# Attention readout and the first expert block of a fused kernel: four entries of a hand-written order moved

## The chip, the cores and the metric

The program runs on one core of one Trainium2 chip. The metric is the device time of one execution in microseconds; the median of the runs of the kernel before is 201.0 us (three runs, 200.04 to 203.24).

## What is computed

Two blocks run one after the other. The first is an attention with a polynomial sketch in place of the softmax. The second takes its output, row by row, to one of eight experts.

```python
def phi(x):                                   # r = 8, head_dim = 32
    a = np.einsum('rd,bhsd->bhsr', S1, x)
    b = np.einsum('rd,bhsd->bhsr', S2, x)
    return np.einsum('bhsi,bhsj->bhsij', a, b).reshape(*x.shape[:-1], r * r)
q_p, k_p = (phi(q), phi(k))                   # q, k, v: (4, 4, 1088, 32)
kv = np.einsum('bhsf,bhsd->bhfd', k_p, v)
z = np.sum(k_p, axis=2)
num = np.einsum('bhsf,bhfd->bhsd', q_p, kv)
den = np.einsum('bhsf,bhf->bhs', q_p, z)[..., None] + 1e-06
x = (num / den) -> rows of (B*S, H*D) = (4352, 128)
...
logits = xn @ en.T / tau;  expert_idx = argmax;  gate_w = softmax prob of that expert
for e in range(8):
    h = np.maximum(x[mask] @ w1[e], 0.0)      # w1: (8, 128, 1024)
    out[mask] = gate_w[mask, None] * (h @ w2[e])
```

## The kernel before, in words

The four batches are worked on in two pairs, number 0 and number 1. The rows of a pair are cut into four tiles of four chunks (named 0 to 3) and a rest (r). For keys and queries of each tile a step turns the tile on TensorE (`ktr`, `qtr`, line 427), sketches it (`kab`, `qab`), copies the sketch out of PSUM and multiplies the two halves into 64 features per head (`kp`, `qp`, line 464). The keys' features meet the values in `kv` (line 530). For the queries of pair 1 the features are turned back, so that features lie on partitions: `trqp` (line 642, TensorE, into PSUM) and `qpT` (lines 648 and 651, ScalarE, PSUM to SBUF). `nd` (line 664, TensorE) multiplies them with the summed keys and values into PSUM tile `ps_big`, which is called the readout here; `x` (lines 677 to 684, VectorE) divides by the denominator and writes the rows `xg` and their router logits. The diff's words are these: "query features turned" is `trqp` with `qpT`, and tile number 2 is the third tile; "second, third readout" are `nd 1 1` and `nd 1 2`.

Behind that come 35 blocks of 128 rows. Block i has its rows fetched by an indirect DMA (`fetch`, line 1047, GpSimd's queue), is turned on TensorE (`turn`, line 1057) and copied to SBUF as `xTb` (line 1059), multiplied with the first weights (`up`, line 1139, into `ps_big`), put through Relu by ScalarE (line 1147), multiplied with the second weights (`down`, lines 1177 and 1182) and scattered to the output (line 1195). `norm` (lines 1152 and 1153) and `shares` (line 1163) make its gate. The first ten blocks hold rows of pair 0 alone, so that block 0 can begin while pair 1 is still read out.

The order of the work on every engine is written out by hand. `HEAD` (line 400), `ORDER` (line 408) and `AFTER_TURN` (line 417) are lists of step names; each step's instructions are emitted in the order of the lists, and the steps of one block get a rank within the block's tick. Each engine runs its instructions in that order and waits where one of them needs a semaphore. The steps of `AFTER_TURN` stand behind the `up` of block 0 and the `turn` of block 1. Which instruction may start is also set by the pools of buffers:

```python
    def ps_small():
        return psum.tile([P, 512], F32, tag="t", bufs=2, name="ps_t")
    def ps_big():
        return psum.tile([P, 2, 512], F32, tag="big", bufs=2, name="ps_big")
...
    def tile_of(n, shape, tag):
        return work.tile(shape, F32, tag=tag if n > 1 else tag + "1",
                         bufs=2 if tag == "both" and n == 1 else 1 if n == 1 else
                         {"both": 4, "qT": 3, "kp": 3}.get(tag, 2), name=tag)
...
            elif c0 // 4 in TWO_BANKS:
                s["ps"] = [ps_one("acc"), ps_one("ab")]
```

So `nd` and `up` take turns in two PSUM buffers `ps_big`, and a new one waits until the reader of the one before the last has done. The turned features `qpT` of whole tiles have two buffers in SBUF. `trqp 2` and `trqp 3` both go through the one buffer `ps_acc` and the one buffer `ps_ab`, so that the later of them waits for ScalarE's copies of the earlier.

At the start of the program the two sketch matrices come in as words of 64-bit numbers, are put together on VectorE (`words`) and turned on TensorE (`sketches`, line 232); VectorE then writes three tiles from that (lines 233 to 236).

Of the kernel before, what the change touches and what calls it, by code (L numbers as in the profile page):

```python
# [72 lines left out]
def kernel(  # L73
# [324 lines left out]


    HEAD = """  # L400
constants; words; norm emb; one columns; clear 0; sketches; ktr0 0; qtr0 0; scale emb; kab0 0; kb0 0; turn emb; pairs 0; kp0 0;
place emb; sec 0 0; ktr0 1; sec 0 1; qtr0 1; prod 0 0; prod 0 1;
kab0 1; kb0 1; kp0 1; lane; ktr0 2; pairs 1; qtr0 2; sec 1 0; sec 1 1; prod 1 0; prod 1 1; ktr0 3; kab0 2; kb0 2;
kp0 2; lanes; qtr0 3; kv0 0; pairs 2; sec 2 0; sec 2 1; prod 2 0; prod 2 1; kab0 3; kb0 3; kp0 3; downs; ktr0 r; qtr0 r; kv0 1;
# [6 lines left out]
qab 0 t; qb 0; kv 3; best 0; place 0; count; qtr 3; qtr r; qp 0;  # L411
take 0; kv 2; kv r; qtr 2; trqp 0; total; split 0; trkv; qab 1 t; qab 3 ab; rest; mark 00; qb 1;
qab r ab; mark 01; find; exp0; kvT; qab 2 acc; sums; kve; qb 2; qpT 0; qb 3; qb r; qp 1; tokens; qp 3; kz;
trqp 1; nd 1 0; fetch0; fetch 1; qp 2; qp r; x 1 0; trqp 3; qpT 1; others; qpT 3; nd 1 1; x 1 1; trqp 2; norm 0; turn 0;
qpT 2; trqp r; qpT r"""
    AFTER_UP = ""
    AFTER_TURN = "nd 1 2; x 1 2; nd 1 3; x 1 3"
    steps = {}

    def turned(tiles, rest, n, tag, parts=1, big=False):  # L420
# [461 lines left out]
    def plan_early():  # L882

        full, upto, w = column("full"), column("upto0"), column("w_early")

        def count():
            tokens_by_expert(((less, ones),), full, spare[0][:, NC * E:(NC + 1) * E])

        def rest():
            nc.vector.tensor_tensor_scan(out=upto[:], data0=ones_e[:], data1=full[:], initial=0.0, op0=ALU.mult, op1=ALU.add)  # L890
            nc.vector.tensor_scalar(w, full, -1.0, float(KEYS), op0=ALU.mult, op1=ALU.add)
            first, early["expert_0"], early["experts"] = blocks(0, upto, w, lane)
            at = first()
            nc.vector.tensor_add(at, at, lane[:, :EARLY])
            early["key"] = at

        def others():
            nc.vector.tensor_scalar_min(c_early[:, 1:], upto, float(EARLY))
            early["took"] = column("took")
            nc.vector.tensor_sub(early["took"], c_early[:, 1:], c_early[:, :E])  # L900
        return count, rest, others
# [303 lines left out]
    def put_at(tick):  # L1205
        def put(after, rank, f):
            at.setdefault(tick + after, []).append((rank, len(at.get(tick + after, ())), f))
        put.tick = tick
        return put
# [11 lines left out]
    count, rest, others = plan_early()  # L1221
# [13 lines left out]
    for i, name in enumerate(x.strip() for x in ORDER.split(";")):  # L1235
        put_at(4)(0, 47.2 + 0.01 * i, steps[name])
    for at_, names in ((30.5, AFTER_UP), (46, AFTER_TURN)):
        for i, name in enumerate(x.strip() for x in names.split(";") if x):
# [3 lines left out]
    count, rest, shared, others, experts, number, start, extra = plan_late()  # L1242
# [118 lines left out]
```

## Time and profile before

| | |
|---|---|
| median of the runs | 201.0 us (200.04 to 203.24) |
| profiled execution, its own time | 200.79 us |
| its span, first to last instruction | 198.8 us |
| TensorE (PE) busy | 186.3 us, 94% of the span |
| ScalarE (ACT), GpSimd (POOL), VectorE (DVE) busy | 106.3, 103.7 and 90.6 us |
| mean granted TensorE clock | 0.991 |

The profile holds one execution. A row of its timeline gives the start on the span's clock, the time from there to the end of the row's last instruction, the engine (PEld is TensorE's weight load), the source line, the operation, output and inputs, how many instructions stand in the row, and in brackets how long the engine had been idle and what ended that. The ends of matmuls are modelled. A float32 matmul of the program stands as two in the trace, a transpose as one. "remote" in brackets means that the profile knows no instruction whose end released the waiting one.

### The profile page before, as it was taken

How to read it: one execution, taken by the hardware profiler on the slowest of the kernel's cores; microseconds unless marked ns; L12 is line 12 of the kernel's file. 1: busy time of each engine (PE TensorE's matmuls, PEld its weight loads, DVE VectorE, ACT ScalarE, POOL GpSimd, SP SyncE). 2: the span in 40 equal slices, each digit the busy share in tenths (PEclk: the TensorE clock that was granted, in tenths of full speed). 3: DMA queues.
4: the chain of work that ended last, by engine and by line, in shares of the span. 5: the costliest groups of instructions: out<-in, count | busy, mean ns of one | idle time of the engine just before them, and what ended most of it. 6: DMA issues, size and time to landing. Idle time of an engine off the chain costs nothing.

```text
span 198.8 us, 7202 instructions
## 1 busy us (share of the span) xinstructions
PE 186.3 (94%) x2701; PEld 176.5 (89%) x2701; DVE 90.6 (46%) x396; ACT 106.3 (53%) x293; POOL 103.7 (52%) x134
## 2 busy tenths in 40 slices
PE   8978999999579997999999999999999999999991
PEld 7657889998478997999999999999999998999990
DVE  6777877899336818994223122221312211123200
ACT  3664443246235517552366564556545596978850
POOL 5110029105715275384588878767687666732442
PEclk9999999999969999999999999999999999999999
DMA  5898999987460688634553979878699799694201
GB/s 142 230 307 232 325 246 296 316 282 200 129 261 0 167 285 325 214 124 129 162 154 83 279 189 277 219 228 231 170 281 273 218 326 230 174 329 108 95 26 33
DMA packets 42598, 41.22 MB, mean 207 GB/s; under 512 B 17625, under 2 KB 36066, under 8 KB 42562
## 3 DMA queue, kind: packets, MB, share of 16 engines
q1 hardware_dynamic: 40272, 36.06, 63.2%
q0 software_dynamic: 2240, 4.67, 7.3%
q8 instruction: 23, 0.38, 0.8%
q14 instruction: 13, 0.11, 0.2%
q10 hardware_dynamic: 50, 0.01, 0.0%
HBM read 34.69 MB, written 6.10 MB: 205 GB/s over the span
## 4 chain that ended last, share of the span: by engine, by line
PE 61%; DMA 18%; DVE 10%; another core or an unknown queue 4%; issue 2%; ACT 2%; SPq 1%; POOLq 1%; ACTq 0%; DVEq 0%
PE ps_big L1139 22%; DMA out_dram<-y,dst_i 12%; PE ps_ab L1177 10%; PE ps_acc L1177 9%; PE ps_big L664 5%; PE ps_acc L530 4%; DMA v<-in_v_dram 4%; DMA k<-in_k_dram 2%; DVE hits L848 1%; PE ps_t L855 1%; PE ps_t L427 1%; PE ps_big L1144 1%; DVE row L775 1%; PE ps_acc L1182 1%
## 5 line engine op out<-in xcount | busy, mean ns | idle before, releaser
L1139 PE MATMUL ps_big<-xTb,wb 128*128 128x128 f32 (+1 forms) x608 | 64.4, 279 | 4.9 <-ACT xTb L1059 4.6
L1139 PEld LDWEIGHTS ps_big<-xTb,wb 128*128 128x128 f32 (+1 forms) x608 | 60.7, 178 | 6.0 <-ACT xTb L1059 5.1
L1195 POOL DMA_INDIRECT out_dram<-y,dst_i x35 | 36.2, 1035 | 41.6 <-ACT sq L1152 11.8
L1147 ACT ACTIVATE hT<-ps_big 128x1024 f32<-128x1024 f32 x35 | 35.8, 1023 | 37.7 <-PE ps_big L1139 21.2
L1047 POOL DMA_INDIRECT xs<-rows,dst_i x35 | 35.6, 1018 | 18.8 <-DVE dst_i L872 11.2
L1166 DVE TENSOR_SCALAR gate<-gate 128x1 f32<-128x1 f32 x35 | 5.2, 148 | 54.0 <-ACT probs L1163 26.7
L1177 PE MATMUL ps_ab<-w_sb,hT 128*128 x208 | 25.6, 276 | 0.0
L1177 PE MATMUL ps_acc<-w_sb,hT 128*128 x208 | 25.4, 275 | 0.0
L1153 POOL TENSOR_TENSOR norm<-norm,half_c 128x1 f32<-128x1 f32 x35 | 21.5, 616 | 6.8 <-ACT sq L1152 6.4
L1177 PEld LDWEIGHTS ps_ab<-w_sb,hT 128*128 128x128 f32 x208 | 24.3, 192 | 0.1
L1177 PEld LDWEIGHTS ps_acc<-w_sb,hT 128*128 128x128 f32 x208 | 24.3, 192 | 0.0
L464 POOL TENSOR_TENSOR kp<-both 128x1024 f32<-128x1024 f32 (+1 forms) x3 | 4.5, 1512 | 16.8 <-ACT both L459 16.8
L1054 DVE STREAM_TRANSPOSE xTb<-held 128x128 f32<-128x128 f32 x22 | 9.2, 416 | 9.0 <-DMA held<-squares 8.1
L1115 ACT COPY v<-w_sb 128x1024 f32 x12 | 12.2, 1039 | 0.5 <-issue 0.4
L1188 ACT ACTIVATE y<-ps_ab,gate 128x128 f32<-128x128 f32 x17 | 6.2, 365 | 9.8 <-PE ps_t L1057 3.4
L1163 ACT ACTIVATE probs<-xs,norm 128x8 f32<-128x8 f32 x35 | 10.3, 296 | 1.3 <-DVE norm L1157 1.3
L1152 ACT ACTIVATE sq<-xs 128x128 f32<-128x128 f32 x35 | 10.6, 302 | 0.1
L1182 PE MATMUL ps_acc<-v,hT 128*64 128x128 f32 (+1 forms) x192 | 10.1, 274 | 0.2 <-issue 0.2
L1182 PEld LDWEIGHTS ps_acc<-v,hT 128*64 128x64 f32 (+1 forms) x192 | 8.8, 128 | 0.9 <-issue 0.4
L1188 ACT ACTIVATE y<-ps_acc,gate 128x128 f32<-128x128 f32 x17 | 6.2, 367 | 6.2 <-issue 3.3
L530 PE MATMUL ps_acc<-v,kp 128*64 128x64 f32 x224 | 7.6, 224 | 1.1 <-DMA v<-in_v_dram 1.1
L530 PEld LDWEIGHTS ps_acc<-v,kp 128*64 128x64 f32 x224 | 7.0, 138 | 1.8 <-issue 1.8
(279 smaller groups left out, 289.6 us busy)
## 6 DMA issues: line engine op xcount, KB each, us to landing
wb<-in_moe_w_dram SPq DMA_DIRECT2D x35, 512.0 KB
w_sb<-in_moe_w_dram SPq DMA_DIRECT2D x16, 256.0 KB
rows<-xg SPq DMA_DIRECT2D x4, 544.0 KB
v<-in_v_dram SPq DMA_DIRECT2D x4, 512.0 KB
k<-in_k_dram SPq DMA_DIRECT2D x3, 512.0 KB
q<-in_q_dram SPq DMA_DIRECT2D x3, 512.0 KB
v<-in_moe_w_dram SPq DMA_DIRECT2D x3, 512.0 KB
squares<-xs SPq DMA_DIRECT2D x22, 64.0 KB
```

What stands on the lines that cost most here:

```text
L530: nc.tensor.matmul(acc[m][u * HALF:(u + 1) * HALF, i, p], s["kp"][:, c - c0, h], bass.AP(tensor=vo.tensor, offset=vo.offset, ap=[list(vo.a ...
L1047: nc.gpsimd.indirect_dma_start(out=xs[i][:], out_offset=None, in_=rows[:2 * S if t == 0 else N + 1], in_offset=bass.IndirectOffsetOnAxis(a ...
L1115: nc.scalar.copy(to, w2_sb[:, bass.ds(e, 1)].rearrange("p o f d -> p (o f d)"))
L1139: nc.tensor.matmul(ps[c:c1, u, j * P:(j + 1) * P], w[:, f * P + c:f * P + c1], x, start=True, stop=True)
L1147: nc.scalar.activation(hT[i], ps, ACT.Relu)
L1152: nc.scalar.activation(sq, xs[i][:, :DM], ACT.Square, accum_out=norms[i])
L1153: nc.gpsimd.tensor_tensor(out=norms[i], in0=norms[i], in1=half_c, op=ALU.pow)
L1163: nc.scalar.activation(p, xs[i][:, DM:], ACT.Exp, scale=norms.pop(i)[:, 0:1], accum_out=gate[i])
L1177: nc.tensor.matmul(ps, h[:, f * P:(f + 1) * P], ws[0][:, f], start=f == 0, stop=f == NF - 1)
L1182: made = nc.tensor.matmul(ps[n0:n1], h[:, f * P + n0:f * P + n1], ws[int(two(i) and n0 > 0)][:, f], start=f == 0, stop=f == NF - 1, skip_g ...
L1188: y_made = nc.scalar.activation(y, ps, ACT.Copy, scale=gate.pop(i)[:, 0:1])
L1195: d = nc.gpsimd.indirect_dma_start(out=out[:, :], out_offset=bass.IndirectOffsetOnAxis(ap=dst_i[t][:, j:j + 1], axis=0), in_=y[:], in_offs ...
```

## The change

Four entries of the lists are moved; no instruction is added, taken away or altered.

```diff
     HEAD = """
-constants; words; norm emb; one columns; clear 0; sketches; ktr0 0; qtr0 0; scale emb; kab0 0; kb0 0; turn emb; pairs 0; kp0 0;
+constants; words; norm emb; one columns; clear 0; ktr0 0; sketches; qtr0 0; scale emb; kab0 0; kb0 0; turn emb; pairs 0; kp0 0;
 place emb; sec 0 0; ktr0 1; sec 0 1; qtr0 1; prod 0 0; prod 0 1;
...
 qab r ab; mark 01; find; exp0; kvT; qab 2 acc; sums; kve; qb 2; qpT 0; qb 3; qb r; qp 1; tokens; qp 3; kz;
-trqp 1; nd 1 0; fetch0; fetch 1; qp 2; qp r; x 1 0; trqp 3; qpT 1; others; qpT 3; nd 1 1; x 1 1; trqp 2; norm 0; turn 0;
-qpT 2; trqp r; qpT r"""
+trqp 1; nd 1 0; fetch0; fetch 1; qp 2; qp r; x 1 0; trqp 3; qpT 1; others; qpT 3; trqp 2; qpT 2; nd 1 1; x 1 1; trqp r; qpT r; norm 0; turn 0; nd 1 2; x 1 2"""
     AFTER_UP = ""
-    AFTER_TURN = "nd 1 2; x 1 2; nd 1 3; x 1 3"
+    AFTER_TURN = "nd 1 3; x 1 3"
```

On TensorE, from the readout `nd 1 0` (`ps_big_1099`) to the end of the readout of pair 1, the kernel before has this (L664 is a readout, L642 turns query features, L1057 turns a block's rows, L1139 is `up`; the first L1057 and the first L1139 belong to block 0):

```order
L664 MATMUL ps_big_1099<-kz1_208,qpT_1077 64x82 x16
L642 MATMUL ps_acc_1137<-ident_87,qp_1086 128x128 x4
L642 MATMUL ps_ab_1138<-ident_87,qp_1086 128x128 x4
L664 MATMUL ps_big_1156<-kz1_208,qpT_1147 64x82 x16
L642 MATMUL ps_acc_1180<-ident_87,qp_1126 128x128 x4
L642 MATMUL ps_ab_1181<-ident_87,qp_1126 128x128 x4
L1057 MATMUL ps_t_1194<-ident_87,xs_1116 128x128
L642 MATMUL ps_t_1201<-ident_87,qp_1128 128x128 x2
L1077 TENSOR_LOAD exp_0_213
L1139 MATMUL ps_big_1211<-xTb_1196,wb_1038 128x128 x8
L1057 MATMUL ps_t_1229<-ident_87,xs_1118 128x128
L664 MATMUL ps_big_1233<-kz1_208,qpT_1198 64x82 x16
```

In the changed kernel, whose source lines are one less, the same stretch reads:

```order
L663 MATMUL ps_big_1099<-kz1_208,qpT_1077 64x82 x16
L641 MATMUL ps_acc_1137<-ident_87,qp_1086 128x128 x4
L641 MATMUL ps_ab_1138<-ident_87,qp_1086 128x128 x4
L641 MATMUL ps_acc_1156<-ident_87,qp_1126 128x128 x4
L641 MATMUL ps_ab_1157<-ident_87,qp_1126 128x128 x4
L663 MATMUL ps_big_1169<-kz1_208,qpT_1147 64x82 x16
L641 MATMUL ps_t_1193<-ident_87,qp_1128 128x128 x2
L1056 MATMUL ps_t_1202<-ident_87,xs_1116 128x128
L663 MATMUL ps_big_1206<-kz1_208,qpT_1166 64x82 x16
L1076 TENSOR_LOAD exp_0_213
L1138 MATMUL ps_big_1235<-xTb_1204,wb_1038 128x128 x8
L1056 MATMUL ps_t_1253<-ident_87,xs_1118 128x128
```

The eight transposes of tile 2 now stand ahead of `nd 1 1`, and the 16 matmuls of `nd 1 2` ahead of the `up` of block 0, which had stood ahead of them. `nd 1 3` stays where it was, behind the `turn` of block 1.

On ScalarE the stretch between the copies of tile 3's turned features and the Relu of block 0 (L1147) reads, before:

```order
L651 COPY qpT_1153<-ps_acc_1137 128x512
L651 COPY qpT_1153<-ps_ab_1138 128x512
L1152 ACTIVATE sq_1190,norm_1191<-xs_1116 128x128
L1059 COPY xTb_1196<-ps_t_1194 128x128
L651 COPY qpT_1198<-ps_acc_1180 128x512
L651 COPY qpT_1198<-ps_ab_1181 128x512
L648 COPY qpT_1204<-ps_t_1201 128x256
L1147 ACTIVATE hT_1212<-ps_big_1211 128x1024
```

and with the change:

```order
L650 COPY qpT_1153<-ps_acc_1137 128x512
L650 COPY qpT_1153<-ps_ab_1138 128x512
L650 COPY qpT_1166<-ps_acc_1156 128x512
L650 COPY qpT_1166<-ps_ab_1157 128x512
L647 COPY qpT_1196<-ps_t_1193 128x256
L1151 ACTIVATE sq_1198,norm_1199<-xs_1116 128x128
L1058 COPY xTb_1204<-ps_t_1202 128x128
L1146 ACTIVATE hT_1236<-ps_big_1235 128x1024
```

The copy `xTb` of block 0 and the square for its norm have gone behind the three copies of turned features. On VectorE `x 1 2` goes ahead of the two instructions of block 0's norm, and nothing else moves. GpSimd's and SyncE's queues hold the same instructions in the same order. At the start of the program TensorE turns the first four key chunks (L427) ahead of the sketches (L232) instead of behind them.

## Rows read from the trace of the kernel before

**Rows 1.** The page's chain of waits: shares of the span by engine.
```profile
PE 61%; DMA 18%; DVE 10%; another core or an unknown queue 4%; issue 2%; ACT 2%; SPq 1%; POOLq 1%; ACTq 0%; DVEq 0%
```

**Rows 2.** Timeline of PE (start us, us, engine, line, operation, count, idle before), 48 to 63 us.
```profile
48.77 0.66 PE L642 MATMUL ps_acc<-ident,qp 128*128 128x128 f32 x4
49.79 1.37 PE L664 MATMUL ps_big<-kz,qpT 128*64 128x82 f32 x32
51.09 0.66 PE L642 MATMUL ps_acc<-ident,qp 128*128 128x128 f32 x4
...
52.02 0.27 PE L1057 MATMUL ps_t<-ident,xs 128*128 128x128 f32 x1
52.12 0.38 PE L642 MATMUL ps_t<-ident,qp 128*128 128x128 f32 x2
56.10 3.68 PE L1139 MATMUL ps_big<-xTb,wb 128*128 128x128 f32 x16 [3.59 <-ACT xTb L1059]
59.62 0.27 PE L1057 MATMUL ps_t<-ident,xs 128*128 128x128 f32 x1
59.82 2.79 PE L664 MATMUL ps_big<-kz,qpT 128*64 128x82 f32 x72
62.87 2.02 PE L1139 MATMUL ps_big<-xTb,wb 128*128 128x128 f32 x16 [0.25 <-PE ps_big L664]
```

**Rows 3.** Timeline of DVE, 54 to 56 us: `x 1 1` from first to last.
```profile
54.26 0.17 DVE L677 TENSOR_SCALAR rc<-ps_big 128x16 f32<-128x16 f32 x1 [2.97 <-remote]
...
55.37 0.28 DVE L683 TENSOR_TENSOR parts<-ps_big,rc 128x128 f32<-128x128 f32 x1
55.68 0.38 DVE L684 TENSOR_REDUCE lg<-parts 128x32 f32<-128x128 f32 x1
```

**Rows 4.** Timeline of ACT, 49 to 61 us.
```profile
49.52 0.59 ACT L651 COPY qpT<-ps_acc 128x512 f32<-128x512 f32 x1 [0.93 <-PE ps_acc L642]
50.00 0.59 ACT L651 COPY qpT<-ps_ab 128x512 f32<-128x512 f32 x1
50.48 0.32 ACT L1152 ACTIVATE sq<-xs 128x128 f32<-128x128 f32 x1
50.69 0.20 ACT L1152 ACTIVATION_READ_ACCUMULATOR sq<-xs 128x1 f32 x1
55.78 0.27 ACT L1059 COPY xTb<-ps_t 128x128 f32<-128x128 f32 x1 [4.89 <-remote]
...
56.90 0.40 ACT L648 COPY qpT<-ps_t 128x256 f32<-128x256 f32 x1
59.82 1.02 ACT L1147 ACTIVATE hT<-ps_big 128x1024 f32<-128x1024 f32 x1 [2.52 <-PE ps_big L1139]
60.74 0.26 ACT L1059 COPY xTb<-ps_t 128x128 f32<-128x128 f32 x1
```

**Rows 5.** Busy time in stretches: bounds, us; PE, PEld, DVE, ACT, POOL busy (count); clock, DMA share, GB/s.
```profile
52.60:56.00 3.40, 0.00 (x0) 0.00 (x0) 1.64 (x6) 0.22 (x2) 2.45 (x3) 1.00 0.89 292
56.30:59.50 3.20, 3.20 (x16) 3.20 (x17) 0.02 (x1) 1.00 (x3) 0.00 (x0) 0.50 0.59 216
...
63.00:194.00 131.00, 129.78 (x1615) 127.60 (x1617) 45.57 (x238) 77.37 (x215) 83.87 (x95) 1.00 0.69 201
15.60:24.00 8.40, 8.40 (x240) 6.94 (x242) 6.46 (x13) 3.42 (x10) 0.00 (x0) 1.00 0.93 271
```

**Rows 6.** Timeline of PE at the program's start.
```profile
4.32 0.28 PE L232 MATMUL ps_ab<-ident,srows 16*128 16x16 f32 x1
4.54 0.85 PE L427 MATMUL ps_t<-ident,k 128*128 128x128 f32 x4
5.22 0.61 PE L427 MATMUL ps_t<-ident,q 128*128 128x128 f32 x4
...
12.18 0.63 PE L427 MATMUL ps_t<-ident,q 128*128 128x128 f32 x4 [0.49 <-DMA q<-in_q_dram]
...
15.54 1.15 PE L530 MATMUL ps_acc<-v,kp 128*64 128x64 f32 x32 [1.09 <-DMA v<-in_v_dram]
```

**Rows 7.** Timeline of POOL, 53 to 55 us, with the norm and the sixth fetch.
```profile
53.50 0.58 POOL L1153 TENSOR_TENSOR norm<-norm,half_c 128x1 f32<-128x1 f32 x1
54.26 0.99 POOL L1047 DMA_INDIRECT xs<-rows,dst_i  x1 [0.18 <-issue]
```

**Rows 8.** Timeline of PE, 74 to 76 us: the only longer gap behind 63 us.
```profile
75.82 0.38 PE L1139 MATMUL ps_big<-xTb,wb 128*128 128x128 f32 x1 [1.02 <-ACT xTb L1059]
```

## The prediction

> **What bounds the kernel now.** I read the chain of waits first: 61% of it are work of PE, TensorE [rows 1], so what PE waits for is what counts. Then the timeline of PE, in which the reader is to see its one long wait [rows 2]: the last work in front of it starts at 52.12 us, the next at 56.10, and in the busy table PE does nothing at all from 52.6 to 56.0 [rows 5]. The `up` of block 0 that follows takes 3.68 us; the `up` of block 1, the same instructions, takes 2.02 [rows 2], and the granted clock in between is 0.50, which is 1.2 GHz instead of 2.4 [rows 5]. So this place costs 3.6 us of idle time and about 1.7 us of half clock. From 63 to 194 us PE is busy for 129.78 of 131.00 us [rows 5], and the one longer gap there is 1.02 us [rows 8]; what is won or lost before the `up` of block 1, which starts at 62.87, is carried to the end nearly whole. That start is the number I work out.
>
> Next I ask who holds PE. It waits for ScalarE's `xTb`, which runs at 55.78 after an idle time of 4.89 us, though the transpose that it reads started at 52.02 and took 0.27 [rows 2, 4]. VectorE's `x 1 1` begins at 54.26, after 2.97 us idle, though the readout it reads ended by its row at 49.79 + 1.37 = 51.16 [rows 2, 3]. Both are put down to "remote": both engines saw TensorE's signal some 3 us after the end that its rows give (54.26 - 51.16 = 3.1; 55.78 - 52.29 = 3.5). The profile doesn't say why. Everything below hangs on what becomes of these two late signals.
>
> **The change part by part.** *Sketches behind the first keys.* The sketches' transpose starts at 4.32, the keys' at 4.54, and the queries' follows at 5.22 [rows 6]. Exchanged, the keys start 0.2 us earlier and the sketches 5.22 - 4.54 = 0.7 us later, and VectorE's three tiles from them as well. What hides that: PE then waits 0.49 us for queries at 12.18 and 1.09 us for values at 15.54, both for DMAs that nothing here moves [rows 6]. Together 1.6 us of slack against 0.7: I count nothing. Without this cover it would cost 0.7; it can't gain, since the DMA at 15.54 ends the stretch either way.
>
> *Turning tile 2 ahead of `nd 1 1`.* It is the same eight transposes, so PE's work stays. But they need `ps_acc` and `ps_ab` free, and ScalarE's second copy of tile 3 ends at 50.00 + 0.59 = 50.59 [rows 4]. The last four transposes (about 0.45 us, from four in 0.5 in the row at 48.77) then end at 51.1, and `nd 1 1` (1.30 us from its start to the next row) at about 52.45 instead of 51.16. In its turn ScalarE may not write tile 2's turned features at once: they have the buffer that `nd 1 1` reads, of two, so all of ScalarE's queue behind them, block 0's square and `xTb` included, waits for the signal of `nd 1 1`.
>
> *From that signal to the first block.* ScalarE: two copies 0.48 + 0.59 = 1.07, the rest's copy 0.35, square and accumulator 0.41, `xTb` 0.26 [rows 4], together 2.1 us. PE meanwhile has the readout `nd 1 2` to do, 1.30 us, after the first 1.07. VectorE's `x 1 1` frees its PSUM buffer for `up` after 55.37 + 0.28 - 54.26 = 1.4 us [rows 3]; that fits below the 2.1. On GpSimd the norm of block 0 and, queued behind it, the sixth fetch [rows 7] come later by as much as the square; that block's `turn` is five ticks away, so nobody waits.
>
> *From `up` of block 0 to `up` of block 1.* Relu starts 0.05 us after `up` ends, and `xTb` of block 1 is done 0.92 + 0.26 = 1.2 us later [rows 4]. PE has a `turn` (0.1 us) and `nd 1 3` to do in that time: 40 of the 72 matmuls that take 2.79 us, so 1.6 us [rows 2]; the buffer that it writes is free once `x 1 2` has read it, 1.4 us after `nd 1 2`. So I take 1.7 us from the end of the one `up` to the start of the next (before: 62.87 - 59.78 = 3.1, with both readouts in it).
>
> *The sum.* I take it that the late signals come at the moments at which they came, 54.24 and 55.7: nothing that is moved is on the DMA queues or on GpSimd's queue up to there. ScalarE copies tile 2 from 54.3 to 55.35, PE does `nd 1 2` from 55.4 to 56.7, ScalarE copies the rest at 55.8 and has `xTb` ready at 56.8. `up` of block 0 runs from 56.85 to 58.65 at full clock, and `up` of block 1 starts at 58.65 + 1.7 = 60.35: 2.5 us earlier than 62.87. The clock is the disputed term. The longest idle stretch of PE falls from 3.6 to 55.4 - 52.7 = 2.7 us. The rows have a gap of 1.09 us with the clock still at 1.00 behind it [rows 5, 6], and one of 3.6 with 0.50 behind it; 2.7 lies between the two. I take full clock, since the 1.3 us of readout separate the gap from the `up`; at half clock `up` takes 3.68 again and the 2.5 become 0.7. That is the lower end of this case. Against the profiled execution's own time the sum is 200.79 - 2.5 = 198.3; that time lies 0.2 below the median of the runs, so I forecast 198.5.
>
> **The rivals.** *The signals come at once.* Then `nd 1 1` ends at 52.45, `nd 1 2` runs from 53.6 to 54.9, `xTb` is ready at 54.55, `up` of block 0 runs from 54.9 to 56.7, that of block 1 starts at 58.4: 4.5 us earlier, 196.5. For it speaks that in all the other waits of [rows 2 and 4] the waiting engine starts at once. Against it speaks that the times of before lie within 200.04 to 203.24, so that nothing of 5 us came and went between its runs. The Trainium skill ("TensorE: Matmul & The Clock Gate", section "The cost: per-tile semaphore tail") gives the signal at the end of a group of matmuls a tail of 25 ns, 4.7 ns a tile and 26.3 ns an increment, which by my estimate is under 0.2 us for `nd 1 1`. By that rule the forecast would be this rival's; the 3.1 us above disagree with it, and I follow the trace.
>
> *The delay belongs to the readout, not to the moment* (the other side). If the signal of `nd 1 1` comes 3.1 us after its end wherever it stands, ScalarE goes on at 55.55, `nd 1 2` runs from 56.65 and PE has idled 3.95 us, longer than the 3.6 that halved the clock. `nd 1 2` then takes 2.6 us, `up` of block 0 about 2.5 with part of it at full clock, and `up` of block 1 starts at about 63.4: 0.5 us late, 201.5. If the signal of `nd 1 2` is late by 3.1 us as well, `x 1 2` starts at 62.35, frees the buffer at 63.75, `nd 1 3` (1.6) follows, and `up` of block 1 starts at 65.35, 2.5 us later than before: 203.5, slower. The old order kept block 0's `xTb` ahead of the copies in ScalarE's queue, the new one puts 1.8 us of copies and square between the signal and `xTb`. The point from which it decides is a delay of some 2.8 us behind `nd 1 1`; below that the new order wins. For it speaks that `x 1 1` and `xTb` were late by nearly the same amount; against it, that the transposes of tile 3 just ahead released ScalarE at 49.52, 0.1 us after their end by the row, 48.77 + 0.66 = 49.43 [rows 2, 4].
>
> *The gap is still long enough to halve the clock.* Late signals as in the forecast, `up` of block 0 at 3.68: 0.7 us gained, 200.3.
>
> **How the numbers follow.** The forecast has a chance of 0.42, signals at once 0.24, the delay that goes with the readout 0.20 (half of it at 201.5, half at 203.5), the halved clock 0.14. Two per cent, about what a measurement of this kernel can tell from no change, is 4.0 us here: faster means below 197.0. Of the signals-at-once case 0.16 lie there, and 0.05 of the forecast's (should the first signal alone come early): 0.21. Slower means above 205.0; the second rival ends at 203.5, so it takes one more late signal: 0.06. Within 2%: 0.73. The range is 196.2 to 202.8: it takes in most of the first rival, the halved clock and the milder half of the slower case. The likeliest case by itself spans 197.2 to 199.8.
>
> **What would show it.** Right: the first `xTb` of ScalarE comes behind three copies, `nd 1 2` stands ahead of the first `up` near 55.4 to 56.7, no 0.50 in the clock behind it, and `up` of block 1 starts near 60.4. The `kv` at 15.54 starts within 0.2 us of that. Wrong: `x 1 1` starts within 0.2 us of the end of `nd 1 1` (first rival), or 3 us after it with the clock at 0.50 behind (second); the longer gaps behind 63 us add up to more than 2 us, so that the gain isn't carried to the end; or PE waits more than 1.1 us at 15.54.

## The result and the profile after

The kernel before takes 200.31 us and the changed kernel 198.72 us, medians of 20 runs each, a difference of 1.6 us. Ratios and intervals, here and below, leave out runs in a slower state (here three of the changed kernel, 199.94 to 200.22 us, the profiled one among them): the ratio is 0.9891, with a 95% interval of 0.9864 to 0.9919. So the change gains 1.6 to 2.7 us on this chip, within 2%. The profiled execution of the changed kernel took 200.22 us (span 198.2), the longest of the twenty; its stretches are read below, its total is not.

I measure the stretch that the prediction speaks of as the time from the start of the readout `nd 1 0` to the start of `up` of block 1. Before it was 62.87 - 47.47 = 15.40 us. After, in the timeline of PE (all line numbers are one less than before):

```profile
46.13 1.36 PE L663 MATMUL ps_big<-kz,qpT 128*64 128x82 f32 x32
48.81 0.66 PE L641 MATMUL ps_acc<-ident,qp 128*128 128x128 f32 x4 [0.29 <-ACT qpT L650]
49.89 1.37 PE L663 MATMUL ps_big<-kz,qpT 128*64 128x82 f32 x32
51.46 0.27 PE L1056 MATMUL ps_t<-ident,xs 128*128 128x128 f32 x1
53.72 2.67 PE L663 MATMUL ps_big<-kz,qpT 128*64 128x82 f32 x32 [1.99 <-ACT qpT L650]
56.32 2.43 PE L1138 MATMUL ps_big<-xTb,wb 128*128 128x128 f32 x16
58.79 1.65 PE L663 MATMUL ps_big<-kz,qpT 128*64 128x82 f32 x40
60.36 2.05 PE L1138 MATMUL ps_big<-xTb,wb 128*128 128x128 f32 x16
```

These answer to [rows 2]: the stretch is 60.36 - 46.13 = 14.23 us, 1.17 less than before. The wait of 3.59 us in front of the first `up` has become one of 1.99 us in front of the third readout. Busy time in stretches, with the columns of [rows 5]:

```profile
52.00:53.60 1.60, 0.00 (x0) 0.00 (x0) 0.50 (x3) 0.52 (x2) 0.15 (x1) 1.00 0.89 297
53.70:57.10 3.40, 3.38 (x35) 3.01 (x36) 1.69 (x6) 1.19 (x5) 1.56 (x2) 0.50 0.87 324
57.20:60.00 2.80, 2.80 (x49) 2.63 (x50) 1.22 (x5) 1.21 (x3) 0.00 (x0) 1.00 0.12 34
```

Behind that wait the granted clock is 0.50 (1.2 GHz) for 3.4 us, as before. It covers the readout (2.67 us instead of 1.37) and the first part of `up` (2.43 instead of 2.05). VectorE's `x 1 1` and ScalarE's queue, in place of [rows 3, 4]; the second fence is ScalarE:

```profile
53.03 0.17 DVE L676 TENSOR_SCALAR rc<-ps_big 128x16 f32<-128x16 f32 x1 [3.07 <-PE ps_t L1056]
```

```profile
53.08 0.59 ACT L650 COPY qpT<-ps_acc 128x512 f32<-128x512 f32 x1 [3.83 <-PE ps_t L1056]
53.56 0.59 ACT L650 COPY qpT<-ps_ab 128x512 f32<-128x512 f32 x1
54.04 0.39 ACT L647 COPY qpT<-ps_t 128x256 f32<-128x256 f32 x1
54.61 0.28 ACT L1058 COPY xTb<-ps_t 128x128 f32<-128x128 f32 x1
```

Both engines wait for the signal of `nd 1 1`, which ended at 51.26 by its row; it comes at 53.0, 1.8 us late (3.1 before). `xTb` now runs in its turn behind three copies and the square.

A signal is an increment of TensorE's semaphore, and the trace also keeps the moments at which that semaphore changed. Here it changed at 53.01, 53.05 and 53.08, for work that by its rows ended at 51.26, 51.62 and 51.73. In the trace before it changed at 54.24, and then at 55.72, 55.76 and 55.80, for work that ended at 51.16, 52.18, 52.29 and 52.51. So it is TensorE's signal itself that is late and not the engines that read it, and held-up signals come close together.

GpSimd's queue, the last fetch of the run of five (before, the fifth ended at 53.48, just ahead of the norm of [rows 7]):

```profile
51.20 0.95 POOL L1046 DMA_INDIRECT xs<-rows,dst_i  x1 [0.30 <-issue]
```

At the program's start, in place of [rows 6]:

```profile
4.18 1.06 PE L426 MATMUL ps_t<-ident,k 128*128 128x128 f32 x4
5.17 0.28 PE L232 MATMUL ps_ab<-ident,srows 16*128 16x16 f32 x1
14.43 1.15 PE L529 MATMUL ps_acc<-v,kp 128*64 128x64 f32 x32
```

The sketches come 0.85 us later than before, and yet the first `kv` starts at 14.43 instead of 15.54: this time it waits for no DMA. These 1.1 us are most of what puts `nd 1 0` 1.3 us earlier (46.13 against 47.47); that the change has no part in it is not shown on this chip, but head_only and gap_only below find none on another. Behind 63 us there are two longer gaps of PE, 3.1 us together, where before had the one of 1.02 [rows 8]:

```profile
98.56 0.60 PE L1138 MATMUL ps_big<-xTb,wb 128*128 128x128 f32 x3 [1.94 <-DVE norm L1155]
181.05 0.27 PE L1143 MATMUL ps_big<-xTb,wb 128*64 128x64 f32 x1 [1.16 <-DVE norm L1155]
```

The first of them lies behind another late signal: `up` and `turn` that ended at 94.73 and 94.84, and a `down` that ended at 96.63, were signalled at 98.16, 98.20 and 98.36.

The chain of waits keeps an entry for what the profile cannot name, 4% before [rows 1] and now:

```profile
PE 67%; DMA 12%; DVE 12%; another core or an unknown queue 3%; ACT 2%; issue 2%; POOLq 1%; ACTq 0%; DVEq 0%
```

### The profile page after: what moved, and what is told of

The parts are those of the page before. It is cut to its first block, busy times and chain, and to the rows that moved or that the text cites. A ratio compares the mean times of both kernels' runs of the same rounds, so it can differ in the third digit from the quotient of the medians.

```text
span 198.2 us, 7204 instructions
## 1 busy us (share of the span) xinstructions
PE 186.2 (94%) x2701; PEld 176.2 (89%) x2701; DVE 89.8 (45%) x396; ACT 106.9 (54%) x293; POOL 104.0 (52%) x134
## 4 chain that ended last, share of the span: by engine, by line
PE 67%; DMA 12%; DVE 12%; another core or an unknown queue 3%; ACT 2%; issue 2%; POOLq 1%; ACTq 0%; DVEq 0%
PE ps_big L1138 21%; DMA out_dram<-y,dst_i 12%; PE ps_ab L1176 9%; PE ps_acc L1176 8%; PE ps_big L663 6%; PE ps_acc L529 4%; PE ps_t L426 3%; PE ps_big L611 2%; PE ps_t L1056 2%; DVE hits L847 1%; PE ps_acc L113 1%; PE ps_ab L447 1%; PE ps_t L854 1%; PE ps_big L1143 1%
## 5 line engine op out<-in xcount | busy, mean ns | idle before, releaser
L1138 PE MATMUL ps_big<-xTb,wb 128*128 128x128 f32 (+1 forms) x608 | 63.1, 276 | 1.9 <-DVE norm L1155 1.9
L1138 PEld LDWEIGHTS ps_big<-xTb,wb 128*128 128x128 f32 (+1 forms) x608 | 59.4, 175 | 2.9 <-DVE norm L1155 2.1
L663 PE MATMUL ps_big<-kz,qpT 128*64 128x82 f32 x144 | 7.5, 262 | 2.0 <-ACT qpT L650 2.0
L663 PEld LDWEIGHTS ps_big<-kz,qpT 128*64 128x64 f32 x144 | 6.5, 156 | 2.9 <-ACT qpT L650 2.4
```

What stands on the lines that cost most here:

```text
L663: nc.tensor.matmul(ps[i * HALF:(i + 1) * HALF, j * NEXT + p * W:j * NEXT + (p + 1) * W], q_[:, p, k_ * P + i * HALF:k_ * P + (i + 1) * HAL ...
L1138: nc.tensor.matmul(ps[c:c1, u, j * P:(j + 1) * P], w[:, f * P + c:f * P + c1], x, start=True, stop=True)
```

## The experiments

They ran on other chips than the result, which turned out to matter more than the change itself. On the first three chips (B: the first four kernels; C: the next four; D: the held kernels) the kernel before takes 192.61, 192.62 and 192.01 us, not 200.3; on a fourth (E) it takes 201.25. The expectations of the first eight were written for 200.3 us, so they are compared by their differences. "Stretch" is the time from `nd 1 0` to `up` of block 1 in each kernel's own profile.

| chip | kernel | ratio to before (95%) | median us | stretch us |
|---|---|---|---|---|
| first | before / changed | 0.9891 (0.9864 to 0.9919) | 200.31 / 198.72 | 15.40 / 14.23 |
| B | head_only (order of before in the stretch) | 0.9994 (0.9962 to 1.0026) | 192.98 | 10.33 |
| B | gap_only | 1.0036 (1.0001 to 1.0071) | 193.41 | 11.17 |
| B | nd_behind | 1.0085 (1.0055 to 1.0114) | 194.05 | 12.21 |
| B | nd_ahead | 1.0029 (0.9995 to 1.0063) | 193.29 | 10.97 |
| C | after_again (the changed kernel) | 1.0044 (1.0012 to 1.0076) | 193.36 | 11.16 |
| C | held_q2 | 1.0004 (0.9966 to 1.0043) | 192.53 | 10.48 |
| C | warm | 1.0084 (1.0046 to 1.0122) | 194.65 | 12.05 |
| C | late_fetch | 1.0186 (1.0122 to 1.0251) | 196.99 | 15.30 |
| D | hold_before | 1.0319 (1.0276 to 1.0361) | 198.31 | 16.27 |
| D | hold_after | 1.0184 (1.0140 to 1.0228) | 196.23 | 14.72 |
| D | hold_q2 | 1.0149 (1.0110 to 1.0188) | 194.88 | 12.52 |
| E | held_q2_again | 0.9856 (0.9804 to 0.9907) | 197.45 | 12.04 |

The stretch explains nearly all of the times: on B and C what a kernel's stretch has over 10.33 is within 0.3 us of what its ratio gives over 192.6 (nd_ahead 0.64 and 0.56; after_again 0.83 and 0.85; nd_behind 1.88 and 1.64; warm 1.72 and 1.62), late_fetch apart.

### One part of the change at a time

head_only:

```diff
-... clear 0; sketches; ktr0 0; qtr0 0; ...
+... clear 0; ktr0 0; sketches; qtr0 0; ...
```

> The kernel before with one entry moved: the first keys are turned ahead of the sketches. Theory G (the gap): the whole gain of the change comes from the stretch between the second readout and the first up; this edit alone gives 200.3 us, within 0.5 of the kernel before, since the later sketches end in waits for DMAs. Theory H (the head): in the profile after, the first kv starts at 14.43 us instead of 15.54 and everything up to the first readout of pair 1 is 1.3 us earlier; if the edit does that, this kernel takes 199.1 us and its first kv starts near 14.4 in the profile. Against H speaks that the wait that ends there is for a DMA.

It is the same as before (0.9994), so theory H falls on this chip. Its stretch has the order of before. PE:

```profile
46.31 1.36 PE L664 MATMUL ps_big<-kz,qpT 128*64 128x82 f32 x32
48.62 1.36 PE L664 MATMUL ps_big<-kz,qpT 128*64 128x82 f32 x32
50.85 0.27 PE L1057 MATMUL ps_t<-ident,xs 128*128 128x128 f32 x1
51.48 2.05 PE L1139 MATMUL ps_big<-xTb,wb 128*128 128x128 f32 x16
56.64 2.02 PE L1139 MATMUL ps_big<-xTb,wb 128*128 128x128 f32 x16 [0.29 <-PE ps_big L664]
```

and VectorE's `x 1 1` with ScalarE's `xTb`:

```profile
50.05 0.16 DVE L677 TENSOR_SCALAR rc<-ps_big 128x16 f32<-128x16 f32 x1
```

```profile
51.16 0.27 ACT L1059 COPY xTb<-ps_t 128x128 f32<-128x128 f32 x1 [1.44 <-PE ps_t L1057]
```

Here no signal is late: `x 1 1` starts 0.07 us after the readout's end at 49.98, `xTb` 0.04 after the transpose's end at 51.12, `up` of block 0 at 51.48 at full clock. The wait of 3.59 us and the half clock of the profile before aren't there on this chip.

gap_only:

```diff
-... clear 0; ktr0 0; sketches; qtr0 0; ...
+... clear 0; sketches; ktr0 0; qtr0 0; ...
```

(against the changed kernel)

> The changed kernel with the sketches put back ahead of the first keys; the moves around the first block stay. Theory G: 198.7 us, as the changed kernel, 1.6 below before. Theory H: 199.9 us, the changed kernel's time and the 1.2 us that the head would give.

It is 0.4% slower than before on B, as the whole change is on C (after_again, below). So the stretch carries all that the change does, as theory G has it, but on these chips with the other sign.

after_again is the changed kernel with no edit:

> The changed kernel as it is, for a second profile. If the late signals, the half clock and the early start of the first kv are fixed traits of this program, x 1 1 starts 1.8 us after the second readout's end, the clock stands at 0.50 near 54 us and the first kv starts at 14.4, as in the first profile. If they vary between executions, one or more differ by over 0.5 us. Time 198.7 us either way.

Two of the three traits are not of the program: on C `x 1 1` starts at once and no 0.50 follows. The third, a first `kv` that doesn't wait, is there again (14.58), but it is so in head_only and gap_only too (14.49 and 14.33), whatever the order at the start. PE and then `x 1 1`:

```profile
47.20 1.37 PE L663 MATMUL ps_big<-kz,qpT 128*64 128x82 f32 x32
49.88 0.66 PE L641 MATMUL ps_acc<-ident,qp 128*128 128x128 f32 x4 [0.30 <-ACT qpT L650]
50.95 1.36 PE L663 MATMUL ps_big<-kz,qpT 128*64 128x82 f32 x32
53.06 1.71 PE L663 MATMUL ps_big<-kz,qpT 128*64 128x82 f32 x32 [0.26 <-ACT qpT L650]
54.69 2.05 PE L1138 MATMUL ps_big<-xTb,wb 128*128 128x128 f32 x16
58.36 2.05 PE L1138 MATMUL ps_big<-xTb,wb 128*128 128x128 f32 x16
```

```profile
52.36 0.17 DVE L676 TENSOR_SCALAR rc<-ps_big 128x16 f32<-128x16 f32 x1 [1.34 <-issue]
```

The rows name most of the 0.83 us that the change costs where signals come at once: 0.30 us of wait for `ps_acc`, which ScalarE is still copying for tile 3; 0.26 us in front of the third readout; and 0.35 us within it (1.71 against 1.36; it starts between ScalarE's two copies, the second of which is done only at 53.49). Against that only the 0.29 us ahead of the second `up` is gone.

nd_behind:

```diff
-... norm 0; turn 0; nd 1 2; x 1 2"""
-    AFTER_TURN = "nd 1 3; x 1 3"
+... norm 0; turn 0"""
+    AFTER_TURN = "nd 1 2; x 1 2; nd 1 3; x 1 3"
```

> The changed kernel with the third readout put back behind the up of block 0; the third tile is still turned early, and its copies still stand ahead of the first block's xTb on ScalarE. Theory A (the gain is the readout done in front of up): the signal of the second readout comes near 53.1 as in the changed kernel, three copies and the square follow, up of block 0 starts near 54.9 after a gap of some 3 us at half clock, two readouts lie again between it and the next up, which takes 3.1 us: up of block 1 starts about 1.2 us later than in the changed kernel, 199.9 us. Theory B (the early turn alone gives the gain, by taking 0.7 us of transposes and 1 us of copies out of the later queue): 198.7 us.

194.05 us, 0.64 above gap_only on the same chip by the medians, and 1.04 by the stretches. The early turn alone (theory B) is the worse half: `up` of block 0 then waits 1.48 us for an `xTb` that stands behind three copies, with nothing in front of it to do:

```profile
53.14 2.05 PE L1138 MATMUL ps_big<-xTb,wb 128*128 128x128 f32 x16 [1.48 <-ACT xTb L1058]
```

This agrees with theory A in direction; its 1.2 us were for the first chip.

nd_ahead:

```diff
-... qpT 3; trqp 2; qpT 2; nd 1 1; x 1 1; trqp r; qpT r; norm 0; turn 0; nd 1 2; x 1 2"""
+... qpT 3; nd 1 1; x 1 1; trqp 2; norm 0; turn 0; qpT 2; trqp r; qpT r; nd 1 2; x 1 2"""
```

> The changed kernel with the third tile turned where it was before (behind the second readout) and the first block's square and xTb ahead of its copies on ScalarE; the third readout stays ahead of up. Theory M (the late signals belong to a moment and nothing in TensorE's order changes them): xTb runs near 55 to 55.8 as before, the two copies follow to 57, the readout runs from 57.1 at half clock for 2.6, up of block 0 near 59.7, and up of block 1 about 1 us later than in the kernel before: 201.3 us. Theory D (the signal is late because of the order behind the second readout, and would come at once in another): 197 us.

0.3% above before, at the edge of no difference. Since no signal was late, it does not tell M from D.

### Where the signals come at once: three edits of the changed kernel

held_q2:

```diff
-            s["qpT"] = tile_of(n, [P, 2, w], "qpT")
+            s["qpT"] = held[:, 2].rearrange(...) if c0 == 8 else tile_of(n, [P, 2, w], "qpT")
```

> The changed kernel with the third tile's turned features written to a free part of the tile held (16 KB a partition, unused here), not to a buffer that the second readout still reads. ScalarE then waits for no signal of that readout. Theory S (what is left of the gap is the wait of ScalarE for the late signal): the copies run at once, the third readout follows the turn of block 0 near 51.7, and up of block 0 waits only for x 1 1, which frees its PSUM buffer 1.4 us after its late start at 53.0: up starts near 54.5 instead of 56.3 and of full clock, 1.8 to 3 us gained, 196.3 us. Theory T (every signal of this stretch is held to about the same moment, 53 to 55, whatever asks for it): xTb of block 0 comes no earlier than 54.6, up as now, 198.5 us.

It can't be told from before (1.0004): the third tile's copies run while `nd 1 1` does, the third readout follows the `turn` without a wait, and of the change's 0.83 us only 0.15 are left in the stretch. There was no late signal to decide between S and T; the run on chip E, below, bears on it.

warm:

```diff
         nc.tensor.transpose(ps[:, :P], xs[i][:, :DM], ident)
+        for _ in range(7 if i == 0 else 0):
+            nc.tensor.matmul(ps[:, 2 * P:3 * P], nought, nought, start=True, stop=True)
```

> The changed kernel with seven more matmuls of zeros (128x128, into columns of a PSUM tile that nothing reads) behind the turn of block 0, so that TensorE works through most of its wait of 2.0 us. By the row of an up, 2.02 us for eight, they take 1.8 us. Theory C (the half clock behind this wait costs time in those executions that have it: in the profile after, the readout took 2.67 us against 1.37 and up 2.43 against 2.02): 197.2 us, no 0.50 in the clock near 54 us and a smaller spread of the times. Rival (the readout and up at half clock lie beside waits that end as late anyway): 198.7 us.

There was no gap of 2.0 us to fill, only the 0.26 of after_again, so the seven matmuls (1.73 us) stand in the way: 1.3 us slower than after_again on the same chip. Theory C is not tested by it.

late_fetch:

```diff
-... nd 1 0; fetch0; fetch 1; qp 2; ... turn 0; nd 1 2; x 1 2"""
+... nd 1 0; fetch0; qp 2; ... turn 0; fetch 1; nd 1 2; x 1 2"""
```

> The changed kernel with the fetches of blocks 1 to 4 (four indirect DMAs back to back on GpSimd) behind the norm of block 0 in GpSimd's queue, so that only one fetch stands in front of the second readout. Theory F (TensorE's signals are late while GpSimd issues indirect DMAs back to back; in both traces every late signal lies in or just behind such a run): x 1 1 starts within 0.3 us of the end of the second readout, the gap ahead of the third readout falls from 2.0 to under 1 us, and later signals near 56 may be late instead; 197.5 us if those cost nothing. Rival (the fetches have no part in it): x 1 1 starts 1.5 to 3 us after the readout's end as now, 198.7 us, or later by what block 1 waits for its rows.

Of F this kernel tells nothing, but after_again does: there the same five fetches run (the last row of them below), and `x 1 1` starts at once at 52.36.

```profile
52.27 0.95 POOL L1046 DMA_INDIRECT xs<-rows,dst_i  x1 [0.30 <-issue]
```

Fetches back to back are thus not enough to make a signal late. What the late fetches cost is seen in PE's row of block 1, which waits for its rows:

```profile
58.75 0.44 PE L1056 MATMUL ps_t<-ident,xs 128*128 128x128 f32 x1 [2.55 <-DMA xs<-rows,dst_i]
```

### The late moments made by hand

On D the signals were replaced by held-up readers: copies and products that nothing reads keep ScalarE and VectorE from taking the signals before the moments of the first chip.

```diff
+ "hold a": n copies nc.scalar.copy(held[:, 3, :1024], held[:, 1, :1024])
+ "hold v": 3 products nc.vector.tensor_mul(held[:, 0], held[:, 1], held[:, 1])
 before:  ... nd 1 1; hold v; x 1 1; trqp 2; norm 0; hold a; turn 0; ...
 changed: ... trqp 2; hold a; qpT 2; nd 1 1; hold v; x 1 1; ...
 hold_q2: ... trqp 2; qpT 2; hold a; nd 1 1; hold v; x 1 1; ... norm 0; hold b; turn 0; ...
```

hold_q2 has the edit of held_q2 besides; "hold b" is one more such copy.

> On the chips of the earlier experiments no signal of TensorE is late and the kernel before takes 192.6 us. This is the kernel before with ScalarE kept busy with copies that nothing reads (5.3 of 0.92 us) ahead of the first xTb, and VectorE with three products ahead of x 1 1, so that x 1 1 begins about 6.8 us and xTb about 8.3 us after the start of the readout nd 1 0, the moments at which the late signals came in the profile before. Theory M (the late signals, at those moments, are all that sets the first chip's stretch apart): up of block 0 comes after an idle time of 3.5 us, the clock is halved behind it, and up of block 1 starts 15.4 us after nd 1 0 instead of 10.3: 197.6 us. Rival (the first chip's gain has another source): see the next kernel.

> The changed kernel held up in the same way: four copies that nothing reads on ScalarE ahead of the third tile's, three products on VectorE ahead of x 1 1, so that both begin 6.8 to 6.9 us after the start of nd 1 0, as in the first profile after. Theory M: the third readout does its work in the held time, up of block 1 starts 14.2 us after nd 1 0 if the clock is halved and 12.7 if not: 196.4 or 194.9 us, that is 1.2 to 2.7 us below the held kernel before, although without the hold the changed kernel is 0.8 us slower. Rival (the change gains nothing in this stretch, and the first chip's 2.2 us come from elsewhere, as from the values that landed 1.1 us earlier): it stays 0.8 us above the held kernel before.

> The changed kernel with the third tile's features in the free part of held, held up at the same moments (ScalarE from behind the third tile's copies to 6.9 us after nd 1 0, xTb not before 8.3, x 1 1 not before 6.8). Theory M: the third readout needs none of the late signals and runs at once, TensorE idles about 1.6 us ahead of up of block 0 and keeps its clock, and up of block 1 starts about 12.3 us after nd 1 0: 194.6 us, below both held kernels. Rival (up waits for x 1 1 and xTb in any case, and the clock falls as well): 196.4 us, as the held changed kernel.

Medians 198.31, 196.23 and 194.88 us; theory M asked for 197.6, 196.4 (at half clock) and 194.6. The held changed kernel is 1.0184 / 1.0319 = 0.987 of the held kernel before by the ratios of the table (0.990 by the medians); the first chip's ratio was 0.9891. Without the hold the same two orders stand 0.4% the other way round. So readers held to these moments are enough to turn the loss into a gain of the first chip's size: the changed order has work to do in the wait that they make. That nothing else adds to the gain on the first chip is likely by this and not shown. PE of the three, one fence each:

```profile
56.38 3.48 PE L1139 MATMUL ps_big<-xTb,wb 128*128 128x128 f32 x16 [4.64 <-ACT xTb L1059]
62.97 1.24 PE L1139 MATMUL ps_big<-xTb,wb 128*128 128x128 f32 x9 [0.29 <-PE ps_big L664]
```

```profile
54.89 1.81 PE L663 MATMUL ps_big<-kz,qpT 128*64 128x82 f32 x32 [2.23 <-ACT qpT L650]
56.63 3.54 PE L1138 MATMUL ps_big<-xTb,wb 128*128 128x128 f32 x16
61.78 2.05 PE L1138 MATMUL ps_big<-xTb,wb 128*128 128x128 f32 x16
```

```profile
51.98 1.36 PE L663 MATMUL ps_big<-kz,held 128*64 128x82 f32 x32
55.31 2.04 PE L1138 MATMUL ps_big<-xTb,wb 128*128 128x128 f32 x16 [1.97 <-ACT xTb L1058]
58.97 2.05 PE L1138 MATMUL ps_big<-xTb,wb 128*128 128x128 f32 x16
```

The hold came out longer than meant: `x 1 1` begins 7.4 us after `nd 1 0` in all three, not 6.8, and `xTb` of the held kernel before 9.4 us after it, not 8.3 (at 56.06; its six copies took 5.78 us). So the pair is a test of the direction and the rough size, not of the third digit.

### held_q2 on a chip with late signals

No edit to held_q2.

> The changed kernel with the third tile's features in the free part of held, once more, in the hope of a chip with late signals. Where the kernel before takes about 192 us (no late signals): within 0.3 us of it, as in the first run of this kernel. Where it takes about 200 us: with late signals of the size seen there, 4 us below it, 196.5 us, by the held kernels' difference of 198.31 - 194.88 = 3.4 us and the 0.5 us by which their clock differs; rival, if the late signals also hold back the third tile's copies: 198.7 us, as the changed kernel.

On E the kernel before takes 201.25 us and held_q2 197.45, a ratio of 0.9856 (0.9804 to 0.9907). The gain is 2.9 us by the ratio; the expected 4 was high. The 2.5 us of the rival are within the interval, so by time alone the two are not apart; the trace tells them apart. ScalarE, VectorE and PE:

```profile
50.21 0.58 ACT L650 COPY held<-ps_acc 128x512 f32<-128x512 f32 x1 [0.26 <-PE ps_acc L641]
53.79 0.37 ACT L647 COPY qpT<-ps_t 128x256 f32<-128x256 f32 x1 [2.51 <-PE ps_t L1056]
```

```profile
53.75 0.17 DVE L676 TENSOR_SCALAR rc<-ps_big 128x16 f32<-128x16 f32 x1 [3.08 <-PE ps_t L1056]
```

```profile
46.83 1.36 PE L663 MATMUL ps_big<-kz,qpT 128*64 128x82 f32 x32
52.36 0.90 PE L663 MATMUL ps_big<-kz,held 128*64 128x82 f32 x13
53.59 0.94 PE L663 MATMUL ps_big<-kz,held 128*64 128x82 f32 x19 [0.32 <-issue]
55.23 2.02 PE L1138 MATMUL ps_big<-xTb,wb 128*128 128x128 f32 x16 [0.70 <-DVE parts L682]
58.87 2.05 PE L1138 MATMUL ps_big<-xTb,wb 128*128 128x128 f32 x16
```

The third tile's copy ran at once at 50.21, the rival's late copy isn't there. `x 1 1` is late again, by 1.8 us (the readout started at 50.59 and took 1.36), and the next copy of ScalarE as well. But the third readout waits for neither, PE idles 0.32 + 0.70 us instead of 1.99, and both `up` run at full clock (2.02 and 2.05). So theory S holds for what is left of the gap. The 0.32 us are an oddity: the readout stops after 13 of its 32 matmuls, with no semaphore to wait for, and goes on at 53.59, just ahead of the late signals (TensorE's semaphore changed at 53.73, 53.77 and 53.80). So in that moment more than the signal was held up. The stretch is 12.04 us, against 14.23 of the changed kernel on the first chip. Whether E and the first chip are the same is not known. held_q2 lies below the changed kernel on C by 0.8 us and below it on D, both held, by 1.35; each of these pairs has intervals that touch, so that it beats the changed kernel is likely and not shown. That it is not measurably slower than before where nothing is late (1.0004) and faster where something is (0.9856), C and E show.

## Why the prediction was right, and where not

**The time.** Forecast 198.5, measured 198.72; within 2% was the likeliest class and is the class. On the first chip the gain of 2.2 us by the ratio is near the forecast's 2.5 (198.5 from 201.0). But they agree in part by luck, as the parts below show, and three of the signs that the prediction named came out against it: the clock was at 0.50 behind the gap, the first `kv` started at 14.43 and not within 0.2 us of 15.54, and the longer gaps behind 63 us add up to 3.1 us, more than the 2 that it named. In the profiled execution the gain is not carried to the end: `up` of block 1 starts 2.5 us earlier (60.36 against 62.87), and the span is 0.6 us shorter.

**The late signals at the same moments: right for the first of them.** The forecast took it that they come when they came, whatever the order. Counted from the start of `nd 1 0`, `x 1 1` began at 54.26 - 47.47 = 6.79 us before, 53.03 - 46.13 = 6.90 after, and 53.75 - 46.83 = 6.92 in held_q2 on E, though `nd 1 1` itself ended at 3.7, 5.1 and 5.1. So the delay does not go with the readout, and the rival that said so ("comes 3.1 us after its end wherever it stands") doesn't fit: it was 1.8 us in the new order. These are three executions, and on two chips that may differ. The second late moment, 8.25 us after `nd 1 0` before (55.72), has no like after: the signal of the `turn` came together with the first, at 53.08. Nothing in the sum hung on it, since `xTb` has to stand behind the copies in any case. The held kernels show that such moments are enough to give the gain.

**The clock: the term that failed, in the profiled execution and, by the mean clocks, in most of the runs.** "I take full clock, since the 1.3 us of readout separate the gap from the `up`." The readout does separate them, but the clock falls at the gap and the readout itself is the first to run at 1.2 GHz. In the profile it cost 1.30 us on the readout and 0.38 on `up`. That the gap was shorter than forecast (1.99 us, not 2.7) didn't prevent it. The stretch therefore gained 1.17 us, not the 2.5 of the sum, and nearer to the fourth case, the halved clock (0.7).

Not every run is like that. Of all the profiles here, the five with a stretch at half clock ahead of the program's last microseconds have a mean granted clock of 0.986 to 0.991 (before, after, late_fetch, hold_before, hold_after), the nine without one 0.994 to 1.000. Of the 20 runs of the changed kernel 12 have 0.985 to 0.991 and 8 have 0.994 to 1.000, none lies between. The 8 have a median of 197.66 us, 2.6 us below the kernel before: the gain of the sum at full clock. Of the 12, the nine that the ratio counts have 198.97 us, 1.3 us below it. So the forecast's disputed term came out both ways, more often the wrong one, and the median lies between. Where in each run the stretch at half clock stood only the profiled one tells. The same is seen on D (hold_after: two runs of six at 1.000, 195.15 and 195.17 us), while all six runs of hold_before and, on E, all eleven of the kernel before have 0.991 or less. Sparing the clock in some of its executions is thus, it seems, a part of what the change gains.

**The start of `up` of block 1: 60.35 forecast, 60.36 measured, by two errors that cancel.** The program reached `nd 1 0` 1.34 us earlier, 1.1 of them since it did not wait for the values, and lost as much in the stretch: 1.68 us by the clock, less what the readout won by starting behind the first of ScalarE's two copies (at 53.72, the second ends at 54.15), where the sum had it wait for both. That agreement is luck. A check of the forecast on the absolute time alone would have called every step right; from `nd 1 0` it is 12.88 forecast and 14.23 measured. That the runs gain 1.6 to 2.7 us where the profiled stretch gained 1.17 is in part the clock's two outcomes above; the rest is not settled, since there is one profile of each kernel on this chip and gaps like those at 98.56 and 181.05 us may come and go as well.

**The head: right to count nothing, though not for the reason.** The cover was the waits for DMAs, 1.6 us. On B these waits were absent in both orders (head_only and gap_only above). There the first `kv` starts at 14.49 in head_only and 14.33 in gap_only: without cover it costs some 0.2 us, not the 0.7 that I gave. The queries' transposes behind the sketches start at 5.45 and 5.44 and don't move.

**"The signals come at once": the mechanism exists, its time was wrong.** I worked it out as 196.5, faster, because I set prompt signals in the new order against late ones in the old. On chips where they are prompt they are so in both orders, and the change is then 0.4% slower. The case that I hadn't set up is a chip on which the wait in [rows 2] doesn't exist. The Trainium skill ("TensorE: Matmul & The Clock Gate", section "The cost: per-tile semaphore tail") gives the signal a tail that I estimated at under 0.2 us; the 0.07 us of B and the 0.05 of C (52.36 against 50.95 + 1.36) agree with it, the 1.8 us of the first chip and E don't.

**What stays open** is why signals are late on the first chip and on E, and not on B, C and D. Each chip of the experiments was used at one time only, so it is not even shown that the chip, and not the hour, makes the difference. In the three traces of the first chip and E, TensorE's semaphore changed more than 0.5 us after the row's end 12 times (before), 10 times (after) and 10 times (held_q2 on E), the first time in the stretch read here and then up to the end; the semaphores of the other engines never did, and in the other eleven traces none did before the program's last microseconds. In the same three traces 13 to 21% of the semaphore changes of TensorE, ScalarE and VectorE are missing from the record (TensorE 127 to 135 of some 157), in the others hardly any. So the recording may have a part in the lateness; no run tests that. Fetches back to back lie ahead of the moment in all of these traces (on the first chip it comes 0.9 us after the last one's end at 52.15, on E 0.9 after 52.85; before, three more late signals, at 99.08 to 99.28, come 0.9 behind three fetches that end at 98.16), but on C they make nothing late. The late fetches were not tried on a chip with late signals. The Trainium skill ("Perfetto Trace Analysis", section "Tensor Engine Instruction (MATMUL, LD_WEIGHTS)") says that the profile's end of a matmul is estimated and that the signal follows PSUM's acknowledgement. No run here shows whether the matmul, the acknowledgement or the signal's way is what took longer; the pause of 0.32 us on E speaks against the signal's way alone.

## What to carry to other kernels

Before filling a wait, ask whether the wait is the program's or the chip's: one that ends 2 to 3 us after the work waited for, and that the profile puts down to "remote" or to an instruction long done, may be absent on the next chip, and the reordering that fills it then costs what its own dependences cost (here 0.8 us). An edit that takes the dependence away, here a third buffer, cost nothing that could be measured where the signal is prompt and gained 1.4% where it is late. And compare stretches from a common mark rather than absolute times: a DMA that landed 1.1 us earlier hid a wrong term here completely.

## What the runs showed of the hardware

- One and the same program takes 192 us on three chips and 200 to 201 us on two runs elsewhere. Of the first chip's 198.8 - 192.4 = 6.4 us of span over head_only on B, 5.07 lie in the one stretch of 15.40 against 10.33 us, and 1.16 ahead of it.
- The clock behind an idle stretch of PE was still at 1.00 after 1.48 us (nd_behind) and 1.97 us (hold_q2), and fell to 0.50 to 0.56 after 1.99 us (changed kernel), 2.55 us (late_fetch, 0.52 from 58.8 to 61.9 us), 3.59 and 4.64 us. In hold_after, with 2.23 us, it fell only behind the readout: 1.81 us for that, then 3.54 for `up`. In busy time by stretches, hold_after:

```profile
54.90:56.60 1.70, 1.57 (x32) 1.27 (x32) 1.28 (x4) 1.16 (x5) 0.57 (x1) 0.93 0.75 236
56.70:60.10 3.40, 3.40 (x17) 3.33 (x17) 1.92 (x7) 0.00 (x0) 0.99 (x1) 0.55 0.59 225
```

  So which work pays for a gap cannot be placed by the gap alone, nor whether any does: by their mean clocks, runs of one kernel on one chip differ in it (hold_after, and the changed kernel). A readout put between the gap and the `up` is no shelter.
- Late signals were TensorE's alone: in three traces 10 to 12 of them came more than 0.5 us after their row's end, up to 3.5 us, and several at a time (55.72, 55.76 and 55.80 us).
